# A pad of 224 bytes in the constants of a fused attention and gated-MLP kernel

## The chip, the cores and the metric

The kernel runs on one core of a Trainium2 chip. The metric is the device time of one execution in microseconds (us). Five engines take part, each with its own instruction stream: TensorE (PE, its weight loads are PEld), VectorE (DVE), ScalarE (ACT), GpSimd (POOL) and SyncE (SP). SP does no arithmetic here: it issues every transfer, and its queue is the queue of the 16 DMA engines. SBUF is the on-chip memory of 128 partitions, in which each buffer is a range of bytes that begins at the same offset in each partition.

## The reference

Eight batches of eight heads with 576 rows of 64; p has 32 rows a head. The result of the attention goes, row by row, through a layer with 1024 hidden columns.

```python
def sm_attn(qq, kk, vv):
    s = scale * np.matmul(qq, kk.transpose(0, 1, 3, 2))
    s = s - np.max(s, axis=-1, keepdims=True)
    a = np.exp(s)
    a = a / (np.sum(a, axis=-1, keepdims=True) + 1e-09)
    return np.matmul(a, vv)
p_packed = sm_attn(p, k, v)
out = sm_attn(q, p_packed, p_packed)
...
h = x @ w_in
e = np.exp(h - np.max(h, axis=-1, keepdims=True))
sm = e / (np.sum(e, axis=-1, keepdims=True) + 1e-09)
solu = h * sm
mu = np.mean(solu, axis=-1, keepdims=True)
var = np.mean((solu - mu) ** 2, axis=-1, keepdims=True)
ln = (solu - mu) / np.sqrt(var + 1e-06) * g_ln
return (ln @ w_out).astype(np.float32)
```

x has 4608 rows of 512; w_in is 512x1024, w_out 1024x512.

## The kernel before, in words

The work falls into eight batches of attention and 36 tiles of 128 rows for the layer. Since p_packed has only 32 rows a head, w_in is multiplied into p_packed once a batch (`z_mm`, line 637), and a tile's h is the attention weights times that product. Matmuls whose two sides are needed with more than 16 bits are done as three 16-bit products of a high and a low part: `first` (line 760) makes h from a2h, a2l and zh, zl with 24 matmuls of 512 columns a tile, and `second` (line 829) makes the output from yT and the constants wch, wcl with 24 more. The pieces are issued by one list written out by hand (ORDER): `perform` takes them in its order and ties each engine's instructions to it. So every engine, and SP's queue of transfers with it, works through a fixed sequence; a transfer that is late holds what stands behind it, and nothing is reordered at run time.

The transfers, all from SP's queue:

- `load_part` (line 454): from batch 2 on for k, from batch 1 on for q, four loads a batch into the buffer raw. Each fills 32 partitions with 72 runs of 128 bytes. DVE then transposes raw in blocks (line 472).
- `load_rows` (lines 155 and 158): the first batches' k and q, in runs of 1024 and 256 bytes, into raw, which PE transposes (lines 166 and 168).
- `load_v_part` (lines 460 and 462): v in runs of 1024 and 256 bytes, into v_sb, read by PE at line 552.
- `load_weights` (line 222): w_in and w_out in runs of 4096 and 8192 bytes, early, into buffers that zh, zl and raw use later.
- `y_turn` (line 807): the transposing transfer, yhl to yT inside SBUF, one a tile, in pieces of 256 bytes. yhl is made at lines 800 and 803; `second` waits for yT.
- `store` (line 836): o_sb to the output, 2048 bytes a row, one a tile; o_sb is made by `output` at line 142 or 144.

```python
def load_part(name, c):
    ...
    blocks = src.rearrange('h (a n t) (e i) -> n e t (h a) i', n=2, t=32, e=2)
    nc.sync.dma_start(st[name].rearrange('p g a i -> p (g a) i')[32 * c:32 * c + 32], blocks[c // 2, c % 2])
...
def y_turn():
    st['yT'] = mlp.tile([P, 2, NFC, P], F16, name='yT', bufs=2)
    nc.sync.dma_start(st['yT'].rearrange('p t c n -> p (t c) n'), st['y'].rearrange('p t f -> p (t f)'), transpose=True)
...
def store():
    nc.sync.dma_start(out[row:row + P, :], st['o'])
```

Buffers are laid out one behind the other in pools, in this order: const (constants, wch, wcl and the weights among them), raws (raw, v_sb), att, par (a2h, a2l, zh, zl), mlp (o_sb, e, u, yT, yhl), small. The last constant is g_size, the absolute values of the gain, 8 numbers of 4 bytes a partition. It is written once (line 337) and read once (line 341).

Of the kernel before, what the change touches and what calls it, by code (L numbers as in the profile page):

```python
# [6 lines left out]
F32 = mybir.dt.float32  # L7
# [100 lines left out]
def packed_attention_solu_kernel(ctx: ExitStack, tc: tile.TileContext, q: bass.AP, k: bass.AP, v: bass.AP, p: bass.AP, w_in: bass.AP, w_out: bass.AP, g_ln: bass.AP, out: bass.AP):  # L108
# [5 lines left out]
    P = 128  # L114
# [3 lines left out]
    NFC = DF // P  # L118
# [5 lines left out]
    const = ctx.enter_context(tc.tile_pool(name='const', bufs=1))  # L124
# [206 lines left out]

    g_abs, gs, w_scale = ([], [], [])

    g_size = const.tile([P, NFC], F32, name='g_size')

    def gain_sizes():
        nc.vector.scalar_tensor_tensor(out=g_size, in0=g_sb, scalar=-1.0, in1=g_sb, op0=ALU.mult, op1=ALU.max)
# [587 lines left out]
```

## Time and profile before

| what | us |
|---|---|
| median of 3 runs | 418.41 |
| lowest, highest of these | 415.17, 423.61 |
| the profiled execution | 420.36 |
| its span, first to last instruction | 418.6 |

The profiled execution is one more run; 1.8 us of it lie outside the span. It stands 0.5% above the median of the three, and the three lie 2% apart. A share of the DMA queue over 100% means that an engine has more than one packet in flight.

### The profile page before, as it was taken

The page shows a single profiled execution, that of the slowest core. Times are in us where ns is not written, and L with a number is a line of the kernel's source. Part 1 is how long each engine was busy: PE and PEld are TensorE (multiplying, and loading weights), DVE is VectorE, ACT ScalarE, POOL GpSimd, SP SyncE. Part 2 cuts the span into 40 slices and gives each one's busy share as a digit, 9 for nine tenths or more (in the row PEclk, how much of TensorE's full clock was granted, in tenths as well). Part 3 has the DMA queues.
Part 4 walks back from the last instruction along what each step waited for, and adds up shares of the span by engine and source line. Part 5 has one row for each costly group of instructions (what it writes and reads, how often), then busy time and mean ns, then how long its engine had stood idle before and what let it go on. Part 6 is the DMA issues. An engine that isn't in the chain of part 4 may idle for free.

```text
span 418.6 us, 8435 instructions
## 1 busy us (share of the span) xinstructions
PE 385.2 (92%) x3236; PEld 186.6 (45%) x3236; DVE 329.6 (79%) x591; ACT 239.9 (57%) x438; POOL 169.6 (41%) x310
## 2 busy tenths in 40 slices
PE   7689698899879799989999999989999999999996
PEld 6355344344334445534445444544444444444442
DVE  2878989779966879888899899779898779648640
ACT  1777878577535656755738637445644555254231
POOL 0023467665453334054713825304038156503340
PEclk9899899899998999999999999999999999999999
DMA  8999999999999999999997679953335414723772
GB/s 223 334 325 220 306 128 188 143 167 154 171 173 169 181 192 206 152 198 187 187 196 132 139 143 163 182 150 78 100 78 103 100 24 103 174 52 77 125 178 101
DMA packets 225560, 67.00 MB, mean 160 GB/s; under 512 B 207856, under 2 KB 219120, under 8 KB 225008
## 3 DMA queue, kind: packets, MB, share of 16 engines
q1 hardware_dynamic: 225520, 66.47, 87.4%
q8 instruction: 25, 0.41, 0.5%
q14 instruction: 15, 0.12, 0.1%
HBM read 37.23 MB, written 9.44 MB: 111 GB/s over the span
## 4 chain that ended last, share of the span: by engine, by line
PE 62%; DMA 19%; DVE 7%; SPq 5%; ACT 2%; issue 2%; POOL 1%; DVEq 0%; ACTq 0%; POOLq 0%
PE pa L829 34%; PE h L760 15%; DMA raw<-in_q_dram 7%; DMA yT<-yhl 4%; DMA out_dram<-o_sb 4%; PE h L166 2%; PE pa L552 2%; DMA v_sb<-in_v_dram 2%; PE h L637 2%; PE h L592 1%; DVE u L789 1%; PE pa L535 1%; SPq L807 1%; DMA raw<-in_k_dram 1%; SPq L454 1%
## 5 line engine op out<-in xcount | busy, mean ns | idle before, releaser
L829 PE MATMUL pa<-wch,yT 128*128 128x512 f16 x576 | 180.1, 383 | 6.4 <-DMA yT<-yhl 3.7
L829 PEld LDWEIGHTS <-yT 128*128 128x128 f16 x864 | 83.7, 99 | 111.3 <-issue 10.8
L829 PE MATMUL pa<-wcl,yT 128*128 128x512 f16 x288 | 110.2, 383 | 0.0
L784 ACT ACTIVATE e<-h,bias,unit 128x1024 f32<-128x1024 f32 x36 | 43.3, 1204 | 34.1 <-DVE bias L144 33.5
L760 PE MATMUL h<-zh,a2h 128*128 128x512 f16 (+1 forms) x160 | 54.8, 381 | 0.3 <-DVE zl L657 0.2
L789 DVE SCALAR_TENSOR_TENSOR u<-e,s_row,h 128x1024 f32<-128x1024 f32 x36 | 45.7, 1272 | 11.5 <-ACT e L784 8.8
L760 PE MATMUL h<-zl,a2h 128*128 128x512 f16 (+1 forms) x160 | 54.6, 379 | 0.0
L760 PE MATMUL h<-zh,a2l 128*128 128x512 f16 (+1 forms) x160 | 54.6, 379 | 0.0
L766 DVE TENSOR_REDUCE nm<-h 128x1 f32<-128x1024 f32 x36 | 43.4, 1210 | 14.0 <-PE h L760 14.0
L803 DVE SCALAR_TENSOR_TENSOR yhl<-u,negmu,yhl 128x1024 f16<-128x1024 f32 x36 | 47.1, 1311 | 3.4 <-ACT yhl L800 3.3
L800 ACT ACTIVATE yhl<-u,negmu 128x1024 f16<-128x1024 f32 x28 | 32.2, 1150 | 22.6 <-DMA yT<-yhl 12.4
L760 PEld LDWEIGHTS <-a2h 128*128 128x128 f16 (+1 forms) x320 | 27.7, 100 | 35.8 <-issue 2.3
L811 ACT ACTIVATE e<-u,negmu 128x1024 f32<-128x1024 f32 x36 | 41.1, 1142 | 0.0
L142 ACT ACTIVATE o_sb<-pa,c_row 128x512 f32<-128x512 f32 x23 | 15.6, 682 | 39.9 <-DMA out_dram<-o_sb 17.8
L620 POOL TENSOR_TENSOR a<-a,sm 128x576 f32<-128x576 f32 x16 | 18.5, 1156 | 38.3 <-DVE sm L617 38.0
L777 POOL TENSOR_SCALAR bound<-nm,unit 128x1 f32<-128x1 f32 x21 | 9.9, 472 | 44.5 <-DVE nm L766 43.0
L676 POOL TENSOR_TENSOR a2l<-s,a2h 128x576 f16<-128x576 f32 x14 | 18.2, 1301 | 22.7 <-ACT a2h L148 12.0
L607 POOL TENSOR_TENSOR s<-s,mx 128x576 f32<-128x576 f32 x15 | 18.4, 1230 | 19.7 <-DVE mx L604 19.7
L472 DVE STREAM_TRANSPOSE qT<-raw 128x576 f32<-128x576 f32 x28 | 20.8, 759 | 6.3 <-DMA raw<-in_q_dram 6.3
L822 POOL TENSOR_TENSOR c_row<-c_row,neg_half 128x1 f32<-128x1 f32 x36 | 22.9, 635 | 3.0
L821 POOL TENSOR_SCALAR c_row<-sq,k_out,s_eps 128x1 f32<-128x1 f32 x36 | 13.5, 374 | 22.4 <-ACT e L811 21.8
L760 PEld LDWEIGHTS <-a2l 128*128 128x128 f16 (+1 forms) x160 | 14.3, 100 | 16.7
(169 smaller groups left out, 593.2 us busy)
## 6 DMA issues: line engine op xcount, KB each, us to landing
out_dram<-o_sb SPq DMA_DIRECT2D x36, 256.0 KB, 3.1
v_sb<-in_v_dram SPq DMA_DIRECT2D x16, 512.0 KB, 5.8
raw<-in_q_dram SPq DMA_DIRECT2D x28, 288.0 KB, 6.2
raw<-in_k_dram SPq DMA_DIRECT2D x24, 288.0 KB, 6.3
raw<-in_moe_w_out_dram SPq DMA_DIRECT2D x2, 1024.0 KB, 7.8
raw<-in_k_dram SPq DMA_DIRECT2D x8, 256.0 KB, 7.2
zh<-in_moe_w_in_dram SPq DMA_DIRECT2D x2, 1024.0 KB, 8.4
zl<-in_moe_w_in_dram SPq DMA_DIRECT2D x2, 1024.0 KB, 10.8
```

The lines of the kernel that those rows point to most:

```text
L472: nc.vector.transpose(out=st[name][:, g], in_=st[raw][:, g].rearrange('p a i -> p (a i)'))
L607: by('su', r).tensor_tensor(out=st['w', r], in0=st['w', r], in1=st['mx', r].unsqueeze(2).broadcast_to([P, NB, J]), op=ALU.subtract)
L620: by('sn', r).tensor_tensor(out=st['a2', r], in0=st['a2', r], in1=st['sm', r].unsqueeze(2).broadcast_to([P, NB, J]), op=ALU.mult)
L760: nc.tensor.matmul(h[rows, 512 * n:512 * n + 512], lhsT=lhsT, rhs=z[:, r, 512 * n:512 * n + 512], start=t == 0, stop=t == end)
L766: nc.vector.tensor_reduce(out=nm, in_=st['h'], axis=AX.X, op=ALU.max, negate=True)
L784: nc.scalar.activation(st['e'], st['h'], AF.Exp, bias=st['bias'], scale=st['unit'][:, 1:2], accum_out=st['se'])
L789: nc.vector.scalar_tensor_tensor(out=st['u'], in0=st['e'], scalar=st['s_row'], in1=st['h'], op0=ALU.mult, op1=ALU.mult, accum_out=st['su'])
L800: nc.scalar.activation(st['y'][:, 0], st['u'], AF.Identity, bias=st['negmu'])
L803: nc.vector.scalar_tensor_tensor(out=st['y'][:, 1], in0=st['u'], scalar=st['negmu'], in1=st['y'][:, 0], op0=ALU.add, op1=ALU.subtract)
L811: nc.scalar.activation(st['e'], st['u'], AF.Square, bias=st['negmu'], accum_out=st['sq'])
L822: nc.gpsimd.tensor_tensor(out=c_row, in0=c_row, in1=neg_half, op=ALU.pow)
L829: nc.tensor.matmul(st['po'], lhsT=st['yT'][:, a, c], rhs=w[:, c], start=c == 0 and t == 0, stop=c == NFC - 1 and t == 2)
```

## The change

g_size is allocated with 64 numbers a partition in place of 8, and the first 8 are used. The two instructions on it keep their shapes. The instructions of PE, DVE, ACT, POOL and SP are the same as before, in the same order. What changes is where everything behind g_size begins: 224 bytes later.

```diff
-    g_size = const.tile([P, NFC], F32, name='g_size')
+    g_size = const.tile([P, 64], F32, name='g_size')[:, :NFC]
```

Where buffers begin in each partition as the two programs are built, in bytes, and the remainder by 512:

```
buffer                      before         after
pT2 (constant)              4768  (160)    4768  (160)
wch (constant)              28320 (160)    28320 (160)
w_hi (constant)             46272 (192)    46272 (192)
g_size (constant)           54528 (256)    54528 (256)
raw, first of 3             54560 (288)    54784 (0)
v_sb                        82208 (288)    82432 (0)
second s2, second a2, a2l   ...   (32)     ...   (256)
zh, zl, o_sb, e, u, yT, yhl ...   (288)    ...   (0)
```

The other two buffers of raw, and kT, qT, e1, e1T, pp, ppT, a2h, are at 288 before and 0 after as well. The destination of the four copies of p (pT2, line 324) and the constants stay where they were.

## Rows read from the trace of the kernel before

**Rows 1.** The page: engines, DMA queue, chain that ended last.

```profile
PE 385.2 (92%) x3236; PEld 186.6 (45%) x3236; DVE 329.6 (79%) x591; ACT 239.9 (57%) x438; POOL 169.6 (41%) x310
...
DMA packets 225560, 67.00 MB, mean 160 GB/s; under 512 B 207856, under 2 KB 219120, under 8 KB 225008
...
q1 hardware_dynamic: 225520, 66.47, 87.4%
...
PE 62%; DMA 19%; DVE 7%; SPq 5%; ACT 2%; issue 2%; POOL 1%; DVEq 0%; ACTq 0%; POOLq 0%
```

**Rows 2.** Windows: stretch, length, busy of each engine, PE clock, DMA share, GB/s.

```profile
0.00:60.00 60.00, 47.10 (x485) 28.88 (x489) 44.11 (x75) 42.49 (x76) 16.59 (x23) 0.94 1.02 262
60.00:270.00 210.00, 195.19 (x1864) 92.65 (x1857) 180.21 (x338) 129.12 (x252) 100.02 (x181) 0.98 1.14 169
270.00:320.00 50.00, 48.20 (x361) 22.82 (x367) 44.18 (x82) 26.57 (x46) 16.29 (x34) 1.00 0.43 108
320.00:418.60 98.60, 94.69 (x544) 42.28 (x538) 61.10 (x100) 41.74 (x67) 36.72 (x74) 1.00 0.46 105
```

**Rows 3.** The chain's transfers after 60 us, and its last run of matmuls: start, us.

```profile
67.06 9.81 DMA raw<-in_q_dram
...
90.06 7.22 DMA v_sb<-in_v_dram
...
101.02 6.33 DMA yT<-yhl
...
123.22 4.92 DMA raw<-in_q_dram
...
133.81 5.52 DMA out_dram<-o_sb
...
174.60 6.25 DMA yT<-yhl
...
192.96 2.98 DMA out_dram<-o_sb
...
206.03 3.84 DMA out_dram<-o_sb
...
255.49 5.85 DMA yT<-yhl
...
269.20 5.65 DMA out_dram<-o_sb
...
388.82 25.91 PE pa L829 x120
```

**Rows 4.** DMA queue from 252.5 to 253.5 us: one load of raw alone, 128-byte packets.

```profile
DMA packets 1656, 0.21 MB, mean 212 GB/s; under 512 B 1656, under 2 KB 1656, under 8 KB 1656
...
q1 hardware_dynamic: 1656, 0.21, 134.3%
```

**Rows 5.** DMA queue from 89.2 to 89.9 us: v alone, 256-byte packets.

```profile
DMA packets 795, 0.20 MB, mean 291 GB/s; under 512 B 795, under 2 KB 795, under 8 KB 795
...
q1 hardware_dynamic: 795, 0.20, 127.8%
```

**Rows 6.** DMA queue from 410 to 415 us: two stores alone, 2048-byte packets.

```profile
DMA packets 288, 0.52 MB, mean 105 GB/s; under 512 B 32, under 2 KB 32, under 8 KB 288
...
q1 hardware_dynamic: 288, 0.52, 27.1%
```

**Rows 7.** DMA queue from 80 to 82.5 us: loads of raw in a burst.

```profile
DMA packets 2422, 0.31 MB, mean 123 GB/s; under 512 B 2422, under 2 KB 2422, under 8 KB 2422
...
q1 hardware_dynamic: 2422, 0.31, 166.2%
```

**Rows 8.** The page's DMA issues: engine, count, KB each, median us to landing.

```profile
out_dram<-o_sb SPq DMA_DIRECT2D x36, 256.0 KB, 3.1
...
raw<-in_q_dram SPq DMA_DIRECT2D x28, 288.0 KB, 6.2
raw<-in_k_dram SPq DMA_DIRECT2D x24, 288.0 KB, 6.3
```

## The prediction

> **What bounds the kernel now.** I read the page first: PE is busy 92% of the span, and the chain that ended last goes 62% through PE and 19%, or 79.5 us, through transfers [rows 1]. At the end PE is at its floor: 120 matmuls of 512 columns in 25.91 us are 215.9 ns each [rows 3], and 512 columns at 2.4 GHz are 213.3. No change of an address can make PE itself more than about 1% faster, so a gain has to come out of PE's idle time, 33.4 us in all.
>
> The windows say where this idle time lies [rows 2]: 12.9 us before 60 us, 14.8 from there to 270, 1.8 up to 320 and 3.9 behind, the last made up by the final tile's output. Up to 270 us the queue's share is over 100%, so the 16 engines nearly always hold a packet; behind it the share falls under half and PE is hardly ever short of work. So the change can pay in the first 270 us alone, where loads, transposing transfers and stores stand in one queue. The chain shows the places: from 67 to 275 us ten transfers lie on it, 58.4 us together [rows 3]. Not all of this is to be had, since most of a transfer's time is not its packets: a load of raw lands 6.2 us after its issue [rows 8], while its 2304 packets, 144 an engine, need 1.39 us at the rate of a load alone (below).
>
> **The change part by part.** The pad itself costs nothing: no instruction is added and none moves, and g_size is read once. There is room for 224 bytes.
>
> Compute: every tile behind g_size begins 224 bytes later, and on every engine the operands began at a multiple of 32 before and do so after. PE's moving operands from wch, which stays, and from zh, which moves, are issued at one rate in the chain's end already. No row shows a DVE, ACT or POOL operation at another remainder, so nothing bounds it but their place: POOL is busy 41%, ACT 57%, DVE 79% [rows 1], and a change of 1% in DVE's 180 us of the stretch from 60 to 270 us [rows 2] would be 1.8 us of an engine with 30 us to spare there. I take 0, with 1 us either way.
>
> Transfers: this is the term that counts. Before, every run of bytes in raw, v_sb, o_sb and yhl starts 32 bytes past a multiple of 256; after, on one, except that every other 128-byte run starts in its middle. What does a start of 32 past cost? Three stretches hold one kind of transfer alone. 1656 packets of 128 bytes take 134.3% of 16 engines for 1 us, 13.0 ns each [rows 4]. 795 packets of 256 bytes take 127.8% for 0.7 us, 18.0 ns [rows 5]. The stores' 256 packets of 2048 bytes take 27.1% for 5 us, 84.7 ns if the 32 small packets among them count nothing and 83.1 if these take 13 ns each [rows 6]. The line through the two larger sizes is 0.0363 to 0.0372 ns a byte, and at 128 bytes it gives 13.2 to 13.3 ns. The larger packets all straddle a multiple of 256; of the 128-byte ones only every other does. So if straddling cost something, the 128-byte packets would lie under the line by half of it. They do, by 0.2 to 0.4 ns: straddling costs 0.4 to 0.8 ns a packet at most. I take 0.6, and 0 as the lower end, since rounding of packet times is of this size. A cost that every packet has alike, straddling or not, would hide in the line's constant of about 8.5 ns; if it is the 32 bytes over, it is 32 x 0.037 = 1.2 ns. That is the upper end for lone transfers.
>
> The sum of it: 225,520 packets [rows 1] are 14,095 an engine; 0.6 ns each are 8.5 us of the 366 us (87.4% of 418.6) that each engine's packets take, 2.3%. On the chain's 79.5 us of transfers that is 1.8 us, if all of it were packets. Since a load's packets are a quarter (1.39 of 6.2 us, alone) to something under half (2.4 us, in a burst), I take half: 0.9 us. What is late next is the same queue's fixed part and DVE.
>
> A rule of the Trainium skill speaks for the change and is larger than my term. The page "DMA: Bandwidth & Descriptors", section "How a descriptor splits into AXI transactions", says that a transaction starts from an address that is a multiple of 256, so that a descriptor that starts elsewhere also pays for the bytes in front of it, in beats of 32. By it a 128-byte run that starts 32 past pays for 5 beats and one that starts 160 past for 9, against 4 and 8 after. [rows 4] hold both of these kinds, and their mean is no longer than the line of the larger packets allows, so this trace shows no sign of the 9; that all packets lose one beat, it can't exclude. Its time is the second rival below.
>
> Against the profiled execution, 420.36 us, the sum gives 419.5; this execution stands 0.5% over the median of the three, and from 418.41 it gives **417.5 us**. My forecast is no change that can be told from none; about 2% is what a measurement of this kernel can tell, since its runs lie 2% apart.
>
> **The rivals.** First, **bursts get their pace back**. In a burst of several loads of raw the same 128-byte packets last 27.4 ns (166.2% of 16 engines for 2.5 us over 2422) and an engine finishes one every 16.5 ns [rows 7], against 9.66 ns alone [rows 4]. A load in a burst thus needs 144 x 6.8 ns = 0.98 us more. If it is the straddling writes that collide there, aligned ones run at the lone pace. There are 52 such loads [rows 8]. If two thirds are in bursts, it is 34 us of the queue; transfers are 58.4 of 210 us of the chain, 28%, so 9.5 us come off, less than PE's 14.8 us of idle time in that stretch: 409 us. With half of the loads it is 7, with all 14. For it speaks that the packets there are of one kind and only 123 GB/s are moved. Against it speaks that loads that straddle as much run at 212 GB/s when alone; what differs is how many loads are outstanding, and the pad leaves that as it was.
>
> Second, **each packet loses 32 bytes' worth**: 1.2 x 14,095 = 16.9 us an engine, 4.6% of 366, or 3.7 us of the chain's transfers in full: 414.7 us. This is what the skill's rule would give. It is still within 2%.
>
> Third, on the other side, **equal beginnings collide**. Before, packets of neighbouring runs begin 32 past a line and spread over two lines; after, all that 16 engines write at a time begin on the same multiples. If lone loads then fall to the pace of bursts, the half of the 52 loads that may run alone lose 26 x 0.98 = 25.5 us of queue, and some 20 transposing transfers of that stretch, 128 packets an engine each, 20 x 0.87 = 17 us; 28% of both is 12 us: 430 us. It decides as soon as the lone loads of 212 GB/s fall under about 150. Nothing in the rows shows that a common beginning hurts: before, too, all of them begin at one remainder.
>
> That the change doesn't do what it says is excluded by the layout for raw, v_sb, o_sb, yT and yhl; only p's copies stay unaligned, and these run once.
>
> **How the numbers follow.** Forecast, little or nothing: 0.66. Second rival, 414.7: 0.13. First rival, 409: 0.14. Third, 430: 0.07. Faster by over 2%, under 410, is the first rival and little besides: 0.14. Slower by over 2%, over 427, is the third: 0.06. Within 2%: 0.80. The likeliest case with its spread of runs (1% each way) reaches from 413 to 422; to hold 8 in 10, the range takes in the second rival and the smaller prices of the first (7 us), and on the upper side the highest run of before: 410 to 424.
>
> **What would show it.** In the changed kernel's page the packets and bytes are the same. The forecast is right in its steps if lone 128-byte packets take 12.4 to 13.0 ns and those of a burst still some 27, the queue's share stays between 85 and 88%, and PE's idle time is within 3 us of 33. The first rival shows as bursts at over 200 GB/s and a share far under 80%, the second as 11.8 ns alone and 83%, the third as lone loads near 125 GB/s. I am wrong if PE's idle time from 60 to 270 us falls under 8 us or grows past 22, or if DVE's or POOL's mean times change by more than 2%, which I took for nothing.

## The result and the profile after

The changed kernel takes 398.44 us (median of four runs, 397.89 to 399.33) against 418.40 before, a ratio of 0.9549 with the interval 0.9491 to 0.9608: 4.5% faster, where 417.5 us and no change were forecast. Two more measurements of the same kernel, each beside its own runs of before, gave 0.9626 and 0.9582, so what follows speaks of some 4%.

The page of the changed kernel, with the lines that answer to [rows 1] and the granted clock by fortieths of the span, shows the same bytes, a DMA share of 73.2% in place of 87.4%, and DMA with 7% of the chain in place of 19%.

```profile
PE 377.9 (95%) x3232; PEld 185.3 (47%) x3236; DVE 329.1 (83%) x591; ACT 239.3 (60%) x438; POOL 170.7 (43%) x310
...
PEclk9989999999999999999999999999999999999999
...
DMA packets 225560, 67.00 MB, mean 169 GB/s; under 512 B 207856, under 2 KB 219120, under 8 KB 225008
...
q1 hardware_dynamic: 225520, 66.47, 73.2%
...
PE 69%; DVE 15%; DMA 7%; issue 3%; ACT 2%; SPq 2%; POOL 1%; DVEq 0%; ACTq 0%; POOLq 0%
```

The windows of the changed kernel, to be laid beside [rows 2] (stretch, length, busy of PE, PEld, DVE, ACT, POOL, PE clock, DMA share, GB/s):

```profile
0.00:60.00 60.00, 48.73 (x495) 29.95 (x500) 46.86 (x80) 43.79 (x82) 19.91 (x26) 0.97 1.00 281
60.00:270.00 210.00, 207.17 (x2045) 100.96 (x2043) 195.93 (x367) 138.89 (x267) 105.11 (x194) 1.00 0.87 178
270.00:320.00 50.00, 49.68 (x310) 22.20 (x309) 43.15 (x76) 26.63 (x42) 19.59 (x36) 1.00 0.31 80
320.00:396.10 76.10, 72.30 (x387) 32.19 (x385) 43.16 (x71) 29.97 (x48) 26.10 (x56) 1.00 0.45 115
```

The span is 22.5 us shorter (418.6 to 396.1). PE's idle time falls from 33.4 to 18.2 us, and 12.0 of these 15.2 us come from the stretch from 60 to 270 us, where PE was idle for 14.8 us and now is for 2.8. The other 7.3 us are PE's busy time, 385.2 to 377.9. Of these, 1.8 us are no gain: at line 260 the trace of the changed kernel holds 12 matmuls and the one before 16. PE's mean granted clock rises from 0.983 to 0.995 of the 2.4 GHz level, which by an estimate is 385.2 x (1 - 0.983/0.995) = 4.6 us; the rest I can't assign. From 60 to 270 us, where waits went, the clock rises from 0.98 to 1.00, and this recurs in the runs below: it is 0.98 or 0.99 there wherever PE is idle for 6.9 us or more, and 0.99 or 1.00 elsewhere. Before 60 us it rises from 0.94 to 0.97 here, but in after2, the same changed kernel, it is 0.91, so that rise can't be put down to the change. DVE, ACT and POOL keep their busy times within 1%.

Which waits went is seen in the transfers. This is the view of DMA issues of the changed kernel (count, KB each, median us to landing); stores landed in 3.1 us before, loads of raw in 6.2 and 6.3 [rows 8]:

```profile
out_dram<-o_sb SPq DMA_DIRECT2D x36, 256.0 KB, 2.6
raw<-in_q_dram SPq DMA_DIRECT2D x28, 288.0 KB, 5.0
raw<-in_k_dram SPq DMA_DIRECT2D x24, 288.0 KB, 4.6
yT<-yhl SPq DMA_TRANSPOSE x36, 3.8
```

and the same view of the kernel before has, for the transposing transfer:

```profile
yT<-yhl SPq DMA_TRANSPOSE x36, 4.6
```

The chain of the changed kernel from 60 to 280 us holds two transfers of 10.4 us together, where [rows 3] had ten of 58.4:

```profile
75.73 5.17 DMA raw<-in_k_dram
...
247.37 5.18 DMA out_dram<-o_sb
```

The group of `second`'s matmuls says it from PE's side. Behind the second bar stands PE's idle time ahead of them, first before, then after; of 6.4 us, 3.7 of them for yT, nothing is left, and a matmul's mean falls from 383 to 379 ns.

```profile
L829 PE MATMUL pa<-wch,yT 128*128 128x512 f16 x576 | 180.1, 383 | 6.4 <-DMA yT<-yhl 3.7 <-ACT o_sb L142 2.7
```

```profile
L829 PE MATMUL pa<-wch,yT 128*128 128x512 f16 x576 | 178.0, 379 | 0.0
```

Last, two rates. From 54 to 57 us the changed kernel has a burst of loads of raw:

```profile
DMA packets 4581, 0.58 MB, mean 194 GB/s; under 512 B 4581, under 2 KB 4581, under 8 KB 4581
...
q1 hardware_dynamic: 4581, 0.58, 122.7%
```

An engine finishes a 128-byte packet every 3000 x 16 / 4581 = 10.5 ns, where it took 16.5 in a burst before [rows 7], and a packet lasts 1.227 x 10.5 = 12.9 ns in place of 27.4. A transposing transfer alone, 256-byte packets, before (320.5 to 322 us) and after (71.5 to 72.5 us):

```profile
DMA packets 1272, 0.33 MB, mean 217 GB/s; under 512 B 1272, under 2 KB 1272, under 8 KB 1272
```

```profile
DMA packets 1133, 0.29 MB, mean 290 GB/s; under 512 B 1133, under 2 KB 1133, under 8 KB 1133
```

One packet per 18.9 ns and engine before, per 14.1 after. So both kinds of transfer that PE waited for became faster. The runs had to tell which property of the addresses does it, and on which buffers it hangs.

### The profile page after: what moved, and what is told of

It is laid out like the page before. It is cut to its first block, busy times and chain, and to the rows that moved or that the text cites. A ratio compares the mean times of both kernels' runs of the same rounds, so it can differ in the third digit from the quotient of the medians.

```text
span 396.1 us, 8431 instructions
## 1 busy us (share of the span) xinstructions
PE 377.9 (95%) x3232; PEld 185.3 (47%) x3236; DVE 329.1 (83%) x591; ACT 239.3 (60%) x438; POOL 170.7 (43%) x310
## 3 DMA queue, kind: packets, MB, share of 16 engines
q1 hardware_dynamic: 225520, 66.47, 73.2%
## 4 chain that ended last, share of the span: by engine, by line
PE 69%; DVE 15%; DMA 7%; issue 3%; ACT 2%; SPq 2%; POOL 1%; DVEq 0%; ACTq 0%; POOLq 0%
PE pa L829 38%; PE h L760 21%; PE pa L552 2%; DMA raw<-in_k_dram 2%; DMA zl<-in_moe_w_out_dram 2%; DVE nm L766 2%; DVE u L789 2%; PE pa L535 1%; DVE yhl L803 1%; DMA out_dram<-o_sb 1%; DMA raw<-in_moe_w_out_dram 1%; PE h L592 1%; DVE s L661 1%; DVE zl L657 1%; SPq L454 1%
## 5 line engine op out<-in xcount | busy, mean ns | idle before, releaser
L829 PE MATMUL pa<-wch,yT 128*128 128x512 f16 x576 | 178.0, 379 | 0.0
L789 DVE SCALAR_TENSOR_TENSOR u<-e,s_row,h 128x1024 f32<-128x1024 f32 x36 | 45.6, 1271 | 11.7 <-ACT e L784 8.9
L760 PEld LDWEIGHTS <-a2h 128*128 128x128 f16 (+1 forms) x320 | 27.7, 100 | 35.8 <-issue 2.3
L620 POOL TENSOR_TENSOR a<-a,sm 128x576 f32<-128x576 f32 x16 | 18.5, 1156 | 32.4 <-DVE sm L617 32.0
L777 POOL TENSOR_SCALAR bound<-nm,unit 128x1 f32<-128x1 f32 x21 | 10.9, 519 | 40.4 <-DVE nm L766 40.3
L821 POOL TENSOR_SCALAR c_row<-sq,k_out,s_eps 128x1 f32<-128x1 f32 x36 | 14.5, 402 | 21.4 <-ACT e L811 20.8
L822 POOL TENSOR_TENSOR c_row<-c_row,neg_half 128x1 f32<-128x1 f32 x36 | 22.0, 611 | 3.0
```

Of the source, the lines that this page charges most:

```text
L620: by('sn', r).tensor_tensor(out=st['a2', r], in0=st['a2', r], in1=st['sm', r].unsqueeze(2).broadcast_to([P, NB, J]), op=ALU.mult)
L760: nc.tensor.matmul(h[rows, 512 * n:512 * n + 512], lhsT=lhsT, rhs=z[:, r, 512 * n:512 * n + 512], start=t == 0, stop=t == end)
L789: nc.vector.scalar_tensor_tensor(out=st['u'], in0=st['e'], scalar=st['s_row'], in1=st['h'], op0=ALU.mult, op1=ALU.mult, accum_out=st['su'])
L822: nc.gpsimd.tensor_tensor(out=c_row, in0=c_row, in1=neg_half, op=ALU.pow)
L829: nc.tensor.matmul(st['po'], lhsT=st['yT'][:, a, c], rhs=w[:, c], start=c == 0 and t == 0, stop=c == NFC - 1 and t == 2)
```

## The experiments

### How far from which multiple

Only the pad was varied, so that all buffers behind it move together. Theory A was that pieces which are not at multiples of 64 bytes cost, B that a packet costs more where its SBUF side straddles a multiple of 256, C that 512 is needed. By B, a shift of 128 makes the 128-byte runs of raw whole and leaves the 256-byte pieces of the transposing transfers straddling.

```diff
-    g_size = const.tile([P, 64], F32, name='g_size')[:, :NFC]
+    g_size = const.tile([P, 72], F32, name='g_size')[:, :NFC]     # r32
+    g_size = const.tile([P, 16], F32, name='g_size')[:, :NFC]     # r64
+    g_size = const.tile([P, 32], F32, name='g_size')[:, :NFC]     # r128
+    g_size = const.tile([P, 128], F32, name='g_size')[:, :NFC]    # r256
```

r32: 

> The pad is 256 bytes, so that everything behind it moves by more than in the change, but begins 32 past a multiple of 512. All three theories: as before, 415 to 424 us, bursts near 27 ns, queue near 87%. If moving the buffers as such, or their distance to the constants, made the gain, it would be near 398.

r64: 

> The pad is 32 bytes, so that raw, v_sb, o_sb, yT and yhl begin 64 past a multiple of 256. Theory A (what counts is whole pieces of 64 bytes): as the change, 398 us, packets of 128 bytes at 13 ns in bursts too, DMA queue 73%. Theory B (what counts is whether a packet straddles a multiple of 256): as before, 412 to 420 us, bursts near 27 ns, queue over 83%. Theory C (512 is needed): as before.

r128: 

> The pad is 96 bytes: the buffers begin 128 past a multiple of 256. Theory A: 398 us, as the change. Theory B: the runs of 128 bytes no longer straddle a multiple of 256, but the 256-byte pieces of the transposing transfers all do, so loads at 13 ns and transposing transfers at 213 GB/s, some 405 to 410 us. Theory C: as before, 418 us.

r256: 

> The pad is 480 bytes: the buffers begin 256 past a multiple of 512. Theories A and B: 398 us, as the change. Theory C: between 405 and 418 us.

| run | begins at | us | ratio, interval | DMA share | raw (q, k), yT, store land after us |
|---|---|---|---|---|---|
| r32 | 32 past 512 | 419.75 | 0.9994 [0.9945, 1.0043] | 85.6% | 6.5, 6.2, 4.6, 3.0 |
| r64 | 64 past 256 | 415.12 | 0.9921 [0.9883, 0.9960] | 85.3% | 6.3, 6.1, 4.7, 3.1 |
| r128 | 128 past 256 | 403.26 | 0.9638 [0.9599, 0.9676] | 77.3% | 5.2, 4.9, 4.5, 3.1 |
| r256 | 256 past 512 | 400.49 | 0.9561 [0.9519, 0.9602] | 72.9% | 5.0, 4.8, 3.8, 2.6 |

r32 is the control: every buffer moves, the remainder stays, and nothing happens. A falls with r64, whose transfers land as late as before (its 0.8% is taken up at the end). r128 does what B says of each kind: raw lands early, yT late. C falls with r256. r128 and r256 share a chip and lie 2.8 us apart, with no run of one within the spread of the other (402.65 to 404.05, 398.72 to 400.71): this is what everything but the 128-byte runs of raw costs when it begins 128 past.

### Which buffer

Each of these is the changed kernel with one buffer, in rawyhl32 two, put back to 32 past a multiple of 256, the others left whole. The pattern is the same for all; the cuts show one allocation of each buffer and leave out the others.

```diff
-                st[name] = raws.tile([P, G, NB, 32], F32, name='raw', bufs=3)
+                st[name] = raws.tile([P, G * NB * 32 + 128], F32, name='raw', bufs=3)[:, 8:8 + G * NB * 32].rearrange(...)   # raw32
-            st['y'] = mlp.tile([P, 2, DF], F16, name='yhl', bufs=2)
+            st['y'] = mlp.tile([P, 2 * DF + 256], F16, name='yhl', bufs=2)[:, 16:16 + 2 * DF].rearrange(...)   # yhl32
```

raw32 (loads of k and q): 

> The changed kernel, with the three buffers of raw alone begun 32 bytes past a multiple of 512 again (each is made 512 bytes larger; all else begins at multiples of 512). If the loads of raw carry the gain: 408 to 415 us, bursts of 128-byte packets near 27 ns, transposing transfers still at 290 GB/s. If the transposing transfers carry it: 398 to 401 us. The run at 128 past gave back 4.8 us with raw's packets whole, so I expect raw to be worth some 10 us.

yhl32 (source of the transposing transfers): 

> The changed kernel, with yhl alone, the source of the transposing transfers, 32 bytes past. If it is reading that pays for straddling: transposing transfers at 213 GB/s and 402 to 404 us. If it is writing: 290 GB/s and 398 to 399 us.

yT32 (their destination): 

> The changed kernel, with yT alone, the destination of the transposing transfers, 32 bytes past. If writing pays: transposing transfers at 213 GB/s and 402 to 404 us. If reading: 290 GB/s and 398 to 399 us.

osb32 (stores): 

> The changed kernel, with o_sb alone, the source of the stores, 32 bytes past. A packet of 2048 bytes straddles eight multiples of 256 in any case and nine pieces in place of eight are 1/8 more at most: 398 to 400 us, stores landing between 2.6 and 3.1 us.

rawyhl32 (the first two together): 

> The changed kernel with raw and yhl both begun 32 past a multiple of 256 again, all else whole. If the two costs add: 398.4 + 11 + 5 = 414 us. If they overlap in the queue: 410 to 412. If each makes the other worse: 418, as before, which would leave nothing for v_sb, o_sb and p.

v32 (loads of v): 

> The changed kernel with v_sb alone begun 32 past a multiple of 256 again. Its packets have 1024 and 256 bytes, 4 and 1 pieces before and 5 and 2 after: 399 to 402 us if a further piece costs some 5 to 9 ns a packet as in the loads and transposing transfers, no difference if only the packets of 128 bytes matter.

The other way round, rest32 is the kernel before with raw and yhl alone made whole, each 224 bytes later inside a larger buffer:

```diff
-                st[name] = raws.tile([P, G, NB, 32], F32, name='raw', bufs=3)
+                st[name] = raws.tile([P, G * NB * 32 + 64], F32, name='raw', bufs=3)[:, 56:56 + G * NB * 32].rearrange(...)
-            st['y'] = mlp.tile([P, 2, DF], F16, name='yhl', bufs=2)
+            st['y'] = mlp.tile([P, 2 * DF + 128], F16, name='yhl', bufs=2)[:, 112:112 + 2 * DF].rearrange(...)
```

rest32: 

> The kernel before with raw and yhl alone begun at multiples of 256, and v_sb, o_sb, yT, the weights' buffers and p's at 32 past as before. If what the two buffers leave of the gain is real: 402 to 406 us. If raw and yhl are all of it: 398 to 401.

The changed kernel itself ran beside them twice more. The runs of one group, as numbered in the table, share a chip and the runs of before. after2: 

> The changed kernel once more, beside the version with whole constants on the same chip: 397.5 to 399.5 us.

after3: 

> The changed kernel, beside these on the same chip: 397.5 to 402.5 us, as in its two other comparisons.

| run (group) | us | ratio, interval | DMA share | raw (q, k), yT, store land after us |
|---|---|---|---|---|
| raw32 (2) | 409.46 | 0.9771 [0.9705, 0.9837] | 83.0% | 6.0, 6.2, 3.9, 2.6 |
| yhl32 (2) | 403.77 | 0.9588 [0.9504, 0.9671] | 74.9% | 5.0, 4.8, 4.5, 3.0 |
| yT32 (2) | 399.73 | 0.9527 [0.9469, 0.9584] | 73.6% | 5.1, 4.8, 3.8, 2.6 |
| osb32 (2) | 400.63 | 0.9547 [0.9486, 0.9607] | 72.5% | 5.1, 4.9, 3.8, 2.6 |
| rawyhl32 (3) | 414.31 | 0.9863 [0.9790, 0.9936] | 84.2% | 6.2, 6.1, 4.7, 2.9 |
| after2 (3) | 402.20 | 0.9626 [0.9582, 0.9671] | 72.4% | 5.0, 4.8, 3.8, 2.6 |
| v32 (4) | 401.55 | 0.9604 [0.9560, 0.9649] | 72.6% | 5.1, 4.9, 3.9, 2.6 |
| rest32 (4) | 401.94 | 0.9607 [0.9567, 0.9646] | 73.7% | 5.1, 4.9, 3.8, 2.6 |
| after3 (4) | 400.16 | 0.9582 [0.9534, 0.9631] | 72.4% | 5.0, 4.9, 3.8, 2.6 |

raw is the larger half: with it alone put back, 2.3% of gain are left of 4.5, its loads land as late as before, and PE is idle for 9.2 us from 60 to 270 us. This is the window of raw32 over that stretch, and then that of rest32, where PE is idle for 3.6:

```profile
60.00:270.00 210.00, 200.81 (x1979) 97.23 (x1977) 188.12 (x351) 133.63 (x259) 99.01 (x182) 0.99 1.08 177
```

```profile
60.00:270.00 210.00, 206.42 (x2040) 100.38 (x2038) 195.07 (x365) 138.19 (x270) 105.28 (x192) 1.00 0.89 180
```

yhl as a source that straddles slows its own transfers (4.5 against 3.8 us); what this costs in time, yhl32's wide interval can't tell from nothing (its profiled execution took 408.57 us, well over its median). The 2.8 us between r128 and r256 are the better figure: since yT as a destination, o_sb and v_sb don't show in the time below, I put them down mainly to yhl, by elimination; the early loads in longer runs were not tried apart. A store lands in 2.6 us in osb32 too, though its rows begin 32 past; it takes 2.9 to 3.1 us in every run of both tables in which yhl straddles, and 2.6 in all others, so its 3.1 us of before came from the transposing transfers in the queue with it. raw and yhl alone give the whole gain within the error (0.9607 beside 0.9582 on one chip). The shares don't add up, though: rawyhl32 keeps 1.4% (0.6 to 2.1) where by rest32 nothing should be left, and its PE is idle for 15.3 us from 60 to 270 us, as long as before. It may be that the other buffers bring this when the queue is late, and nothing measurable when it is not; that is argued, not shown.

One version went further: the constants pT0, pT2, wch, wcl and the identity at multiples of 512 too.

```diff
-    g_sb = const.tile([P, NFC], F32, name='g_sb')
+    g_sb = const.tile([P, 96], F32, name='g_sb')[:, :NFC]
-    g_size = const.tile([P, 64], F32, name='g_size')[:, :NFC]
+    g_size = const.tile([P, 104], F32, name='g_size')[:, :NFC]
```

best: 

> The changed kernel with g_sb padded too, so that the constants from pT0 to ones_f begin at multiples of 256 as well: the destination of the four copies of p, wch and wcl, w_in_sb and ident. Straddling now costs only in p's copies, which run once, around 46 us, and weigh under 3 us there: 396 to 398.5 us. If the start of a matmul's moving operand counted (wch and wcl were 160 past), the 864 matmuls at line 829 would come closer than 215.9 ns, and it would be under 396.

400.20 us, 0.9572 [0.9525, 0.9619]; the changed kernel beside it had 0.9626 [0.9582, 0.9671]. The two are not told apart, so no version here beats the changed kernel.

### The price of one packet

Two kernels hold transfers alone, group by group, each group waiting for the one before; all arithmetic of the reference is left out. The loads are those of `load_part`, 2304 runs of 128 bytes each. `four` lays the runs end to end from 0, 32, 64 or 128 past a multiple of 256, so that at 32 and 64 every other run straddles one and at 0 and 128 none. `gap` lays the runs 256 bytes apart from 0 or 32 past (none straddles) or from 160 past (every one does). yTa to yTf are transposing transfers.

```diff
+    close('four0', q, 2, 0, range(4)); close('four32', k, 3, 32, range(4))
+    close('four64', q, 3, 64, range(4)); close('four128', k, 4, 128, range(4))
+    apart('gap0', q, 4, 0); apart('gap32', k, 5, 32); apart('gap160', q, 5, 160)
+    for n, (a, b) in enumerate(((0, 0), (32, 0), (64, 0), (128, 0), (256, 0), (0, 32))):   # source, destination of yTa..yTf
```

probe: 

> A kernel that leaves out all arithmetic and only issues transfers, in groups that each wait for the group before: loads in runs of 128 bytes like those of raw, one alone at 0 and at 32 past a multiple of 256, four at once at 0, 32, 64 and 128 past, four at once with a gap of 128 bytes behind each run (begun at 0, at 32, where no run straddles, and at 160, where each does), two at once at 32, four at once into the same 32 partitions at 32; then one transposing transfer at a time with its source at 0, 32, 64, 128 and 256 past and once with its destination at 32; then four stores at once in runs of 128 bytes with gaps, begun at 0, 32 and 160, and of 2048 bytes at 0 and 32. Theory B (straddling a multiple of 256 is what costs): four at once run at about 210 GB/s at 0, 128 and in the gapped layout at 0 and at 32, at 125 to 145 at 32 and 64, and slower still, 90 to 110, where each run straddles; the lone load at 32 at 210. Theory A' (any start off a multiple of 64 costs in a burst): gapped at 32 as slow as at 160. Transposing transfers: 290 GB/s at 0 and 256, 213 at 32, 64 and 128; 290 with the destination at 32.

SP's timeline of the probe (start, us of issuing, what; a group's time is the distance to the next start). In order: four at 0, 32, 64, 128; gap at 0, 32, 160; a pair that only closes gap's last; and, further on, stores in runs of 128 bytes set 256 apart, four from 0 and four from 32 past (none straddles), then four from 160 past (every one does), and long stores that close these.

```profile
10.75 5.18 SPq L49 DMA_DIRECT2D four<-in_q_dram  x4
18.95 5.90 SPq L49 DMA_DIRECT2D four<-in_k_dram  x4
29.82 5.74 SPq L49 DMA_DIRECT2D four<-in_q_dram  x4
40.25 4.98 SPq L49 DMA_DIRECT2D four<-in_k_dram  x4
48.47 5.40 SPq L55 DMA_DIRECT2D gap<-in_q_dram  x4
56.87 4.98 SPq L55 DMA_DIRECT2D gap<-in_k_dram  x4
64.99 6.55 SPq L55 DMA_DIRECT2D gap<-in_q_dram  x4
77.30 1.72 SPq L49 DMA_DIRECT2D two<-in_k_dram  x2
...
118.69 12.13 SPq L90 DMA_DIRECT2D out_dram<-osrc  x8
134.43 7.19 SPq L90 DMA_DIRECT2D out_dram<-ocross  x4
145.78 5.90 SPq L96 DMA_DIRECT2D out_dram<-ocross  x8
```

Four loads take 8.2, 10.9, 10.4 and 8.2 us end to end, and 8.4, 8.1 and 12.3 us set apart. Whole packets take 8.1 to 8.4 us wherever they begin, half of them straddling 10.4 to 10.9, all of them 12.3. Short reads of SBUF pay too: the eight stores that don't straddle take 15.7 us, 7.9 for four, and the four that do 11.4. In mid-burst the queue shows it as follows: gap at 32 (60 to 63 us), then gap at 160 (69 to 72 us).

```profile
DMA packets 4299, 0.55 MB, mean 182 GB/s; under 512 B 4299, under 2 KB 4299, under 8 KB 4299
...
q1 hardware_dynamic: 4299, 0.55, 114.8%
...
DMA packets 2505, 0.32 MB, mean 106 GB/s; under 512 B 2505, under 2 KB 2505, under 8 KB 2505
...
q1 hardware_dynamic: 2505, 0.32, 175.1%
```

11.2 ns a packet and engine against 19.2. For the transposing transfers the windows are of one microsecond each: source at 0, at 32, at 64, and destination at 32.

```profile
DMA packets 1132, 0.29 MB, mean 290 GB/s; under 512 B 1132, under 2 KB 1132, under 8 KB 1132
...
DMA packets 839, 0.21 MB, mean 215 GB/s; under 512 B 839, under 2 KB 839, under 8 KB 839
...
DMA packets 857, 0.22 MB, mean 219 GB/s; under 512 B 857, under 2 KB 857, under 8 KB 857
...
DMA packets 1133, 0.29 MB, mean 290 GB/s; under 512 B 1133, under 2 KB 1133, under 8 KB 1133
```

14.1 ns, 19.1 at 32, 18.7 at 64, and 14.1 with the destination at 32. The source at 128 gives 839 packets from 109 to 110 us, as at 32. The second of the two kernels asked what a load that is alone pays, since the prediction was built on such loads:

```diff
+    apart('ga', q, 1, 32); apart('gb', k, 1, 160)             # each of the four loads waits for the one before
+    close('la', q, 2, 0, [0]); close('lb', k, 2, 32, [0])     # one load, end to end
+    close('lc', q, 3, 0, range(2)); close('ld', k, 3, 32, range(2))
```

probe2: 

> A kernel that leaves out all arithmetic and only issues loads in runs of 128 bytes: first four loads one at a time with a gap behind each run where none straddles, then four one at a time where each does, then one, two and three at once, at 0 and at 32 past. If a straddling load pays only when another is outstanding beside it: the lone straddling loads land as soon as the others, 3.1 to 3.3 us. If writes fall behind and only the first packets look unharmed: their packets keep 13 ns at first, but each lands later, by about the 9 ns that a straddling packet costs times 144, 1.3 us; and one, two and three at 32 land 0.6, 1.7 and 2.7 us later than those at 0.

The single-buffer view of it gives the time to landing for ga (none straddles), gb (all), la (none), lb (every other one), lc (two loads, none) and ld (two, every other one), in this order:

```profile
DMA to landing us min/median/max: 3.0/3.1/3.2
...
DMA to landing us min/median/max: 4.1/4.1/4.1
...
DMA to landing us min/median/max: 3.1/3.1/3.1
...
DMA to landing us min/median/max: 3.8/3.8/3.8
...
DMA to landing us min/median/max: 3.1/3.9/4.7
...
DMA to landing us min/median/max: 4.2/5.0/5.8
```

And the queue over all of la (32.7 to 36 us) and over all of lb (36 to 40 us):

```profile
q1 hardware_dynamic: 2320, 0.29, 56.4%
...
q1 hardware_dynamic: 2320, 0.29, 46.9%
```

56.4% of 16 engines for 3.3 us over 2320 packets are 12.8 ns each, 46.9% for 4 us are 12.9. By packet times la and lb are the same load; by landing, lb is 0.7 us later. This is what the prediction could not see. The late part lies behind the last packet: la's packets run from 33.6 to 35.5 us and it lands at 35.8, lb's run from 36.8 to 38.7, as long, and it lands at 39.6. In its last 0.9 us no packet is left (38.7 to 39.6 us):

```profile
DMA packets 0, 0.00 MB, mean 0 GB/s; under 512 B 0, under 2 KB 0, under 8 KB 0
```

Where every packet straddles, even a lone load's packets are longer. This is the queue over the first load of ga (3.8 to 6.8 us, 12.8 ns a packet) and over that of gb (16.3 to 20.3 us, 17.2 ns):

```profile
q1 hardware_dynamic: 2320, 0.29, 62.0%
...
q1 hardware_dynamic: 2320, 0.29, 62.2%
```

The price comes late in the load, though. In the probe's gap at 160, too, the queue starts at the pace of whole packets (66.4 to 66.9 us) before it falls to the 106 GB/s shown above:

```profile
DMA packets 821, 0.11 MB, mean 210 GB/s; under 512 B 821, under 2 KB 821, under 8 KB 821
```

So 210 GB/s for a while says nothing of straddling, and [rows 4] were such a stretch, 212 GB/s in a lone load of which every other packet straddles.

## Why the prediction was wrong

**The bound** was read rightly in its place: the time came off before 270 us, from PE's idle time behind transfers, and DVE, ACT and POOL kept their busy times (the mean of DVE's line 789 went from 1272 to 1271 ns, POOL's line 620 stayed at 1156). One sentence there was too tight: "no change of an address can make PE itself more than about 1% faster". PE's busy time fell by 7.3 us, 1.9%; 1.8 us of it are matmuls missing from the trace, and 4.6, by the estimate above, are its clock.

**The step that failed** is the price of straddling, "0.4 to 0.8 ns a packet at most", and the 0.9 us made of it. It put lone 128-byte packets, half of them straddling, on a line through larger ones, and took the smooth line as proof that straddling is nearly free. The sum of its packets' times is a wrong measure of such a load: la and lb have 12.8 and 12.9 ns a packet and land 0.7 us apart. A load with every packet straddling lands 1.0 us later than a whole one, and its packets do show it (17.2 ns against 12.8), but the kernel before has no such pair to compare. In bursts, where PE's waits come from, the price is 19.2 - 11.2 = 8 ns for a packet that straddles (7.3 by the whole groups: 12.3 - 8.1 us over 576 packets an engine), and for a transposing piece it is 5 ns: about ten times the term.

**The rule that was weighed** was set aside on the same reading. That packets which straddle are the dear ones, the runs bear out: 8.4 and 8.1 us for gap at 0 and at 32, 12.3 for gap at 160. The section "How a descriptor splits into AXI transactions" of the Trainium skill's page "DMA: Bandwidth & Descriptors" counts beats of 32 bytes from the multiple of 256 below a packet's start; worked out by it, these three need 4, 5 and 9 beats. So its 9 was there to be found; but the fifth beat cost nothing here, nor did the 8 that it gives to every other run of four at 0 (8.2 us). Nor do beats give the size for the transposing pieces: by the same working they need 8 at 0, 9 at 32, 10 at 64 and 12 at 128, while the runs have 14.1, 19.1, 18.7 and 19.1 ns. What fits all of these, to some 5%, is that a second piece costs, however many bytes of it are used.

**The first rival**, "bursts get their pace back", at 0.14, is what happened, if not by loads that collide: gb pays alone, 4.1 us against 3.1. It foretold bursts over 200 GB/s (194 measured) and a share far under 80% (73.2%). The argument set against it, that "loads that straddle as much run at 212 GB/s when alone", is the failed step again. Its price of 9.5 us was too small although its 6.8 ns a packet in a burst was right (16.5 - 10.5 = 6.0 measured). It left out the 36 transposing transfers (128 packets an engine each, 36 x 128 x 4.8 ns = 22 us of the queue) and PE's clock, and took 28% of the queue's gain for the chain. PE's idle time from 60 to 270 us alone gave 12.0 us.

**The second rival**, 32 bytes' worth for every packet, falls with gap at 0 and 32 alike. **The third**, that equal beginnings collide, falls with the result itself: all buffers begin alike and a transposing transfer runs at 290 GB/s.

**The signs** that I named did their work: I had written that I am wrong if PE's idle time from 60 to 270 us falls under 8 us, and it is 2.8. The other one, a mean time of POOL or DVE that changes by over 2%, came up in small groups of POOL (line 777 from 472 to 519 ns, line 821 from 374 to 402), but not with the change: r32, which begins as before, has 402 at line 821, and raw32, where all but raw begins as after, has 469 at line 777.

**Open** are what happens between the last packet of a straddling load and its landing, why bursts with half of the packets straddling take 16.5 ns and not the mean of 11.2 and 19.2, r64's 0.8% (in the probe four loads at 64 take 10.4 us and at 32 10.9, each measured once), rawyhl32's 1.4%, and how the gain divides between raw and yhl: with the other one whole, raw costs some 2.2% (raw32) and yhl about 2.8 us (r128 beside r256).

## What to carry to other kernels

Where short runs of 128 or 256 bytes fill the DMA queue, look where the buffers that they are loaded into, or transposed out of, begin by 256: one small constant ahead of them in the pools can shift them all, and whether a run crosses a multiple of 256 is worked out on paper. Judge a transfer by its landing and by the rate of a burst, not by how long the packets of a lone one take. And when the rows that a term is fitted to all share the suspected property, the fit can't price it: [rows 4 to 6] held not one transfer without straddling runs.

## What I had not expected of the hardware

- A 128-byte write whose SBUF side straddles a multiple of 256 costs 19.2 ns an engine in a burst against 11.2; beginning 32 or 128 past the multiple without crossing one costs nothing (8.1 to 8.4 us for four loads). Reads of SBUF by stores in runs of 128 bytes pay too, 11.4 us for four against 7.9.
- A transposing transfer pays on its source side alone: 290 GB/s from whole pieces, 215 to 219 from straddling ones, 290 with the destination 32 past.
- A lone load of which every other packet straddles keeps its packet times (12.9 ns beside 12.8) and lands 0.7 us later, all of it behind the last packet. Where every packet straddles, the load begins at the full pace (210 GB/s) and slows down later.
- Where waits went, PE's granted clock rose too, from 0.98 to 1.00 between 60 and 270 us (0.983 to 0.995 over the span, by an estimate 4.6 us beyond the idle time). That the waits had lowered it is the likely reading; no run varied it alone.
